# Channel attention and two FFNs on one core: three weight units converted in the head, four leftover groups at other places

## The chip, the cores and the metric

One core of a Trainium2 chip. The metric is the device time of one execution in microseconds (us). TensorE (PE) multiplies, VectorE (DVE) and ScalarE (ACT) do the elementwise work, GpSimd (POOL) helps at a few places, and the queue of SyncE (SP) issues every load and store.

## The reference, cut to what matters

```python
qn = q / (np.linalg.norm(q, axis=1, keepdims=True) + 1e-06)   # q, k, v: (1, 6016, 256)
kn = k / (np.linalg.norm(k, axis=1, keepdims=True) + 1e-06)
s = kn.transpose(0, 2, 1) @ qn / tau                          # 256 x 256
a = softmax(s)                                                # exp(s - max) / (sum + 1e-09)
x = v @ a                                                     # 6016 x 256
h = x @ w_in1;  x = (h * np.clip(h + 3.0, 0.0, 6.0) / 6.0) @ w_out1     # 256 -> 2048 -> 256
h = x @ w_in2;  out = np.maximum(h, 0.0) ** 2 @ w_out2
```

## The kernel before

Every product is made of three passes: operands are split into a high part (a cast on ACT) and a rest (a subtraction on DVE), and PE runs high x high, rest x high, high x rest (`passes`, L310 to L312).

The **head** reads q and k in groups of two blocks of 128 tokens (`GROUPS`, tiles `qk`, tags `wo0` to `wo7`, so 8 buffers, each 512 KB). For every one of 47 blocks ACT squares it into PSUM (L296), DVE adds the square to one of two running sums (L297), and PE adds its outer product to the two halves of `s` (`score`, L300). The last ten blocks' second halves are left for later (`late`, `DEFER`).

Then comes the **chain from the norms to M1**: PE sums over partitions (`nrm`, L385), DVE and ACT make reciprocal norms (L391 to L409), PE spreads them (`rq_ps`, L410), ACT copies that (L417), `softmax(0)` and `softmax(1)` scale, take the maximum and exponentiate, PE transposes (`et_ps`, L437), and ACT and DVE split the transposed result. M1 is the softmax times the first 512 columns of `w_in1` (`m1_half`): four half products of three passes each, 12 matmuls, whose casts and rests (`m1_out`, L476, L478) are the weights `wa_0` that the first FFN multiplies x by. `late` scores stand on PE after `nrm` (six of them, `LATE_AT`) and after `rq_ps` (four). `keep_busy` puts matmuls without use into PE's waits.

The weights arrive as 64-bit floats and are **converted in units**: `unit` loads one and returns five steps, on ACT an absolute value, a copy and at the end a cast of the high part, on DVE two TENSOR_SCALAR, a SCALAR_TENSOR_TENSOR, an integer add (L167) and the rest: five DVE instructions. Units are `wi1_0` to `wi1_7` and `wo1_0` to `wo1_7`. In the head only `wi1_0` is converted (`EARLY`, `EARLY_AT`), `wi1_1` and `wo1_0` stand in the chain, and 13 others in the first pair.

The **first pair** (`steps`) is a loop over 32 steps. A step has one product `h` (6 matmuls), ACT's `r` (L628), DVE's `g` (L630), the split into `gs`, and two groups `acc` (6 matmuls) that lag by `LAG` = 2 steps. `issue` is called twice a step and issues the conversion steps that `START` and `DENSE` put at that place. At steps 5, 13 and 21 another M1 part is made. After the last step four groups are left (`pending`); they are put into free slots of the first unit of the next pair, a Strassen unit (`strassen`) of 15 slots. In that unit the bank `y` collects B11, T2, T1 and B22, and ACT copies it out after each of the first three (`sa`, `su`, `se`, L766) before PE may add the next.

Of the kernel before, what the change touches and what calls it, by code (L numbers as in the profile page):

```python
# [8 lines left out]
F32 = mybir.dt.float32  # L9
# [17 lines left out]
NU = KF // 2  # L27
GROUPS = [1] + [2] * 23
DEFER = 10
LATE_AT = 6  # L30
LAG = 2
AHEAD = 3
BUSY = (6, 2, 2, 3)
M1_LEAD = 3
EARLY = 12
TAU_AT = 20
EARLY_AT = {15: (0, 1), 16: (2,), 18: (3, 4)}


START = [-5, -3, 0, 3, 6] + [9 + 4 * k for k in range(9)]  # L40
DENSE = 5
SIGN = -(2 ** 31)
APART = 2.6
APART_FIRST = 3.2
SLOTS = 15

B11, B21, T2, T3, T1, B22, T4 = range(7)
# [8 lines left out]
def attention_then_two_ffns(  # L56
# [230 lines left out]

    s_ps = [ps_acc.tile([P, C], F32, tag="acc", name=f"s{i}") for i in range(KC)]

    sums = [small(2 * C) for _ in range(2)]  # L290
    for x in sums:
        nc.vector.memset(x, 0.0)

    def squares(t, x):
        sq = bank([P, 2 * C], f"sq{t}")
        nc.scalar.activation(sq, x, AF.Square)  # L296
        nc.vector.tensor_tensor(out=sums[t % 2], in0=sq, in1=sums[t % 2], op=ALU.add)  # L297

    def score(t, x, i):
        nc.tensor.matmul(  # L300
# [13 lines left out]
    with tc.manual_schedule():  # L314
# [8 lines left out]
        pre = []  # L323
        t = 0
        for gi, n in enumerate(GROUPS):
            src = wpool.tile([P, 1024], F32, tag=f"wo{gi % NU}", name=f"qk{gi}")[:, :2 * n * C]
            nc.sync.dma_start(
                out=src.rearrange("p (t x c) -> p t x c", t=n, x=2), in_=qk[:, t:t + n, :, :]
            )
            if gi == EARLY:  # L330
                pre.append(unit("wi1", 0, raw1[0]))
            for st in EARLY_AT.get(gi, ()):
                pre[0][st]()
# [17 lines left out]
        et = [hpool.tile([P, KC, C], F32R, tag="o", bufs=4, name=f"et{s}") for s in ("h", "l")]  # L351

        order = [
            ("wo1", 0), ("wi1", 2), ("wo1", 1), ("wi1", 3), ("wo1", 2), ("wi1", 4), ("wo1", 3), ("wi1", 5),
            ("wo1", 4), ("wi1", 6), ("wo1", 5), ("wi1", 7), ("wo1", 6), ("wo1", 7),
        ]
        loaded = []

        def feed():
            k = len(loaded)  # L360
            if k < len(order):
                which, u = order[k]
                loaded.append(unit(which, u, raw1[u] if which == "wi1" and u < len(raw1) else None))
# [4 lines left out]
            for k in range(KC):  # L368
                nc.sync.dma_start(out=raw[k][:, :, :w], in_=(vt[p] if j == 0 else x2_d[p])[:, 2 * k:2 * k + 2, :w])

        pre.append(unit("wi1", 1, raw1[1]))
        raw0 = [gpool.tile([P, 2, WMAX], F32, tag="g", name=f"v0_{k}") for k in range(KC)]
        load_x(0, 0, raw0)
        for _ in range(AHEAD):
            feed()


        for st in range(4):
            pre[1][st]()


        nrm = ps_acc.tile([P, 4], F32, tag="acc", name="nrm")
        for b in range(4):
            for m, x in enumerate(sums):
# [125 lines left out]
        operands = {}  # L510
        raws = {}

        def operand(j, p, r):

            at = j * NP + p
            if r in (B11, B21) and at % 2:
                t = wpool.tile([P, 2, WMAX], F32R, tag=f"b{2 + r}", name=f"x{j}_{p}_{r}")
            elif r == T2 and at % 2:
                t = ops.tile([P, 2, WMAX], F32R, tag="opx", name=f"x{j}_{p}_{r}")
            else:  # L520
                t = ops.tile([P, 2, WMAX], F32R, tag=f"op{r}", name=f"x{j}_{p}_{r}")
            t = t[:, :, :WIDTHS[p]]
            operands[j, p, r] = [t[:, i, :] for i in range(2)]
            return operands[j, p, r]


        x0 = {}

        def split_first(k):
            w = WIDTHS[0]  # L530
            for n in range(2):
                hi, lo = x0[k, n] = operand(0, 0, ((B11, T3), (B21, B22))[k][n])
                split(hi, lo, raw0[k][:, n, :w])
# [440 lines left out]
```

## Time and profile before

| | |
|---|---|
| median of 3 runs | 1046.49 us (1046.17 to 1046.52) |
| profiled execution | 1046.23 us, of which the span of its instructions is 1044.1 us |
| busy share of the span | PE 99%, DVE 83%, ACT 64%, POOL 3% |
| granted TensorE clock | 1.000 in every slice |
| loads of the head | qk 23 x 512 KB and 1 x 256 KB |

The page's busy shares average over very different stages. PE's 99% counts a matmul until its modelled end, so short waits hardly show in it; they are read from the starts of two matmuls in a row.

### The profile page before, as it was taken

Reading aid. Unit: us, or ns where it says so; the run is one execution under the profiler, and the core shown is the slowest. Engines: PE = TensorE matmul, PEld = TensorE weight load, DVE = VectorE, ACT = ScalarE, POOL = GpSimd, SP = SyncE. Lnnn points to the kernel's source line nnn. Section 1 sums busy time; section 2 is a strip of 40 time slices with the busy share of each in tenths; the row PEclk is TensorE's granted clock in tenths of the full one; section 3 lists DMA queues with packets and bytes.
Section 4 is the critical chain, followed back from the end, with each engine's and each line's share of the span. In section 5 each row is a group of like instructions: output and inputs, shape, how many; then the busy total and the mean of one; then the engine's idle time right before and its main releaser. Section 6 shows DMA issues by size and latency. Waiting matters only on the chain.

```text
span 1044.1 us, 12995 instructions
## 1 busy us (share of the span) xinstructions
PE 1033.6 (99%) x4630; PEld 865.3 (83%) x4630; DVE 863.0 (83%) x1461; ACT 665.6 (64%) x1200; POOL 29.9 (3%) x33
## 2 busy tenths in 40 slices
PE   9999999999999999999999999999999999999998
PEld 8867787888888888888998888888888888888997
DVE  7899868889989989988987788778688678778765
ACT  7687777788878778777876455445455455445443
POOL 0012240000000000000000000000000000000000
PEclk9999999999999999999999999999999999999999
DMA  9911204003403402222665002002001100200100
GB/s 371 344 40 41 81 1 142 1 1 116 157 0 116 156 1 111 82 76 92 227 225 187 1 1 80 1 1 69 13 1 40 42 1 1 75 1 1 41 1 36
DMA packets 25936, 77.64 MB, mean 74 GB/s; under 512 B 2832, under 2 KB 4880, under 8 KB 25872
## 3 DMA queue, kind: packets, MB, share of 16 engines
q1 hardware_dynamic: 25872, 76.82, 21.0%
q8 instruction: 36, 0.59, 0.2%
q14 instruction: 28, 0.23, 0.1%
HBM read 52.95 MB, written 23.86 MB: 74 GB/s over the span
## 4 chain that ended last, share of the span: by engine, by line
PE 88%; DVE 7%; ACT 4%; issue 1%; DMA 1%; SPq 0%; ACTq 0%
PE acc L312 15%; PE acc L311 15%; PE acc L310 15%; PE y L310 7%; PE y L311 7%; PE y L312 7%; PE q L311 4%; PE q L310 4%; PE q L312 4%; PE s L300 3%; PE x L312 2%; PE x L310 2%; PE x L311 2%; DVE gs L125 2%; DVE g L630 1%
## 5 line engine op out<-in xcount | busy, mean ns | idle before, releaser
L125 DVE TENSOR_TENSOR gs<-g,gs 128x512 fp32r<-128x512 f32 (+1 forms) x384 | 260.4, 678 | 55.6 <-ACT gs L793 46.1
L312 PE MATMUL acc<-gs,wo 128*128 128x512 f32 (+1 forms) x768 | 296.8, 386 | 0.8 <-DVE gs L125 0.6
L310 PE MATMUL acc<-gs,wo 128*128 128x512 f32 (+1 forms) x768 | 296.2, 386 | 0.9 <-ACT gs L123 0.9
L311 PE MATMUL acc<-gs,wo 128*128 128x512 f32 (+1 forms) x768 | 295.9, 385 | 0.0
L793 ACT CAST gs<-g 128x512 fp32r<-128x512 f32 (+1 forms) x352 | 208.6, 613 | 31.0 <-DVE g L784 22.0
L312 PEld LDWEIGHTS acc<-gs,wo 128*128 128x128 f32 x768 | 144.2, 188 | 30.8 <-DVE gs L125 4.0
L310 PEld LDWEIGHTS acc<-gs,wo 128*128 128x128 f32 x768 | 144.2, 188 | 28.5 <-ACT gs L123 2.0
L311 PEld LDWEIGHTS acc<-gs,wo 128*128 128x128 f32 x768 | 144.2, 188 | 26.6
L766 ACT COPY se<-y 128x512 f32<-128x512 f32 (+1 forms) x88 | 50.7, 576 | 121.3 <-PE y L312 121.2
L770 DVE TENSOR_TENSOR h<-q,se 128x512 f32<-128x512 f32 (+1 forms) x88 | 59.5, 676 | 63.1 <-ACT se L766 62.6
L766 ACT COPY su<-y 128x512 f32<-128x512 f32 (+1 forms) x88 | 50.7, 576 | 87.1 <-PE y L312 76.4
L789 DVE SCALAR_TENSOR_TENSOR g<-h 128x512 f32<-128x512 f32 (+1 forms) x144 | 97.0, 673 | 0.0
L776 ACT ACTIVATE r<-h,three 128x512 f32<-128x512 f32 (+1 forms) x120 | 85.5, 713 | 8.6 <-DVE h L770 8.2
L784 DVE SCALAR_TENSOR_TENSOR g<-r,h 128x512 f32<-128x512 f32 (+1 forms) x120 | 80.6, 672 | 3.8 <-ACT r L776 3.8
L778 ACT ACTIVATE r<-y 128x512 f32<-128x512 f32 (+1 forms) x48 | 28.3, 590 | 62.7 <-PE y L312 62.7
L770 DVE TENSOR_TENSOR h<-q,su 128x512 f32<-128x512 f32 (+1 forms) x88 | 59.4, 675 | 1.4
L770 DVE TENSOR_TENSOR h<-x,sa 128x512 f32<-128x512 f32 (+1 forms) x88 | 59.1, 672 | 0.0
L766 ACT COPY sa<-y 128x512 f32<-128x512 f32 (+1 forms) x88 | 50.7, 576 | 6.8 <-PE y L312 0.7
L789 DVE SCALAR_TENSOR_TENSOR g<-y,r 128x512 f32<-128x512 f32 (+1 forms) x48 | 32.7, 681 | 23.7 <-ACT r L778 23.1
L300 PE MATMUL s<-qk 128*128 128x256 f32 x188 | 41.7, 381 | 0.8 <-DMA qk<-in_qk 0.8
L300 PEld LDWEIGHTS s<-qk 128*128 128x128 f32 x188 | 35.5, 191 | 6.1 <-DMA qk<-in_qk 1.5
L310 PE MATMUL y<-x,wa_0h 128*128 128x512 f32 (+1 forms) x88 | 34.0, 386 | 0.7 <-ACT se L766 0.7
(241 smaller groups left out, 1761.6 us busy)
## 6 DMA issues: line engine op xcount, KB each, us to landing
qk<-in_qk SPq DMA_DIRECT2D x23, 512.0 KB, 7.0
wo<-in_w_out SPq DMA_DIRECT2D x16, 512.0 KB, 5.2
wi<-in_w_in SPq DMA_DIRECT2D x10, 512.0 KB, 4.6
x2d<-o SPq DMA_DIRECT2D x20, 256.0 KB, 2.4
raw<-x2d SPq DMA_DIRECT2D x10, 512.0 KB, 5.6
out<-o SPq DMA_DIRECT2D x20, 256.0 KB, 2.2
raw<-in_vt SPq DMA_DIRECT2D x8, 512.0 KB, 5.9
wo2d<-wo2s SPq DMA_DIRECT2D x8, 512.0 KB, 2.9
```

Source lines behind the costliest of these rows:

```text
L125: eng.tensor_tensor(out=lo, in0=x, in1=f32(hi), op=ALU.subtract)
L300: nc.tensor.matmul(s_ps[i], lhsT=x[:, C + i * P:C + (i + 1) * P], rhs=x[:, :C], start=(t == 0), stop=(t == NT - 1))
L310: nc.tensor.matmul(ps, lhsT=ah, rhs=bh, start=first, stop=False, skip_group_check=more)
L311: nc.tensor.matmul(ps, lhsT=al, rhs=bh, start=False, stop=False, skip_group_check=more)
L312: nc.tensor.matmul(ps, lhsT=ah, rhs=bl, start=False, stop=last, skip_group_check=more)
L766: nc.scalar.copy(s[tag], s["y"])
L770: nc.vector.tensor_tensor(out=s[which], in0=s[ps], in1=s[tag], op=ALU.add)
L776: nc.scalar.activation(s["r" + which], h, AF.Relu, bias=three)
L778: nc.scalar.activation(s["r" + which], h, AF.Relu)
L784: nc.vector.scalar_tensor_tensor(out=g, in0=s["r" + which], scalar=6.0, in1=h, op0=ALU.min, op1=ALU.mult)
L789: nc.vector.scalar_tensor_tensor(out=g, in0=h, scalar=0.0, in1=r, op0=ALU.max, op1=ALU.mult)
L793: nc.scalar.copy(gs[which][0], s["g" + which])
```

## The change

`wi1_0`, `wi1_1` and `wo1_0` are all converted in the head, and loaded between the qk groups 6 and 7, 9 and 10, 12 and 13. The qk tiles keep off tag `wo0` (it now holds `wo1_0`), so they have 7 buffers. The squares of 13 blocks go to SBUF and are added by POOL to a third sum, which DVE adds to the first one at block 41. The table load for Exp stands right behind the square root. Two of the four splits of the first x stand before the norms, one after `rest(0)`, one after M1. Both transposes stand before M1 on PE. The third `keep_busy` goes, and `late` is divided five and five. In the first pair 13 units are issued as before, in another order and at other places, and the four leftover groups stand at slots 1, 8, 11, 12 instead of 3, 4, 6, 8.

```diff
-LATE_AT = 6
+LATE_AT = 5
-BUSY = (6, 2, 2, 3)
+BUSY = (6, 2, 2)
-EARLY = 12
+EARLY = ((6, "wi1", 0), (9, "wi1", 1), (12, "wo1", 0))
+EARLY_AT = (3, 3, 4, 5, 6)
-EARLY_AT = {15: (0, 1), 16: (2,), 18: (3, 4)}
+POOL_UNTIL = 39
+JOIN = 41
-START = [-5, -3, 0, 3, 6] + [9 + 4 * k for k in range(9)]
-DENSE = 5
+START = [-1, 2, 5, 8, 11, 14, 17, 22, 26, 30, 34, 39, 45]
+DENSE = 3
+LEFT_AT = (1, 8, 11, 12)
...
     def squares(t, x):
+        if t % 3 == 1 and t < POOL_UNTIL:
+            sq = hpool.tile([P, 2 * C], F32, tag="r", name=f"sq{t}")
+            nc.scalar.activation(sq, x, AF.Square)
+            nc.gpsimd.tensor_tensor(out=sums[2], in0=sq, in1=sums[2], op=ALU.add)
+        else:
...
+        if t == JOIN:
+            nc.vector.tensor_tensor(out=sums[0], in0=sums[2], in1=sums[0], op=ALU.add)
...
-            src = wpool.tile([P, 1024], F32, tag=f"wo{gi % NU}", name=f"qk{gi}")[:, :2 * n * C]
+            src = wpool.tile([P, 1024], F32, tag=f"wo{1 + gi % (NU - 1)}", name=f"qk{gi}")[:, :2 * n * C]
...
         order = [
-            ("wo1", 0), ("wi1", 2), ("wo1", 1), ("wi1", 3), ("wo1", 2), ("wi1", 4), ("wo1", 3), ("wi1", 5),
-            ("wo1", 4), ("wi1", 6), ("wo1", 5), ("wi1", 7), ("wo1", 6), ("wo1", 7),
+            ("wi1", 2), ("wi1", 3), ("wo1", 1), ("wo1", 2), ("wi1", 4), ("wi1", 5), ("wo1", 3), ("wo1", 4),
+            ("wi1", 6), ("wo1", 5), ("wi1", 7), ("wo1", 6), ("wo1", 7),
         ]
...
-        pre.append(unit("wi1", 1, raw1[1]))
...
-        for st in range(4):
-            pre[1][st]()
+        split_first(0)
...
         nc.scalar.activation(root, x2n, AF.Sqrt, scale=2.0 ** -10)
-        pre[1][4](0)
+        nc.scalar.activation(warm, ones[:, 0:1], AF.Exp)
+        loaded[0][0]()
...
         e0 = softmax(0)
         keep_busy(BUSY[1], "busy1")
-        loaded[0][2]()
         transposed(0, *e0)
         e1 = softmax(1)
-        loaded[0][3]()
-        loaded[0][4](0)
+        row_sums(0, *e0)
         rest(0, *e0)
-        loaded[0][4](1)
-        feed()
-        row_sums(0, *e0)
+        split_first(1, 0)
         keep_busy(BUSY[2], "busy2")
-        m1_half(0, 0, 0)
         transposed(1, *e1)
         rest(1, *e1)
         row_sums(1, *e1)
+        m1_half(0, 0, 0)
         m1_half(0, 0, 1)
-        for k in range(KC):
-            split_first(k)
-        loaded[1][0]()
+        split_first(1, 1)
         m1_out(0, 0)
...
-        free = sorted(set(range(SLOTS)) - {x % SLOTS for x in PLACE})
-        for x, go in zip(free, [(n, f, d, gs) for n, f, gs in pending for d in range(KC)]):
+        for x, go in zip(LEFT_AT, [(n, f, d, gs) for n, f, gs in pending for d in range(KC)], strict=True):
```

How the instructions stand, at three places. ACT from the square root to the first cast of the transposed softmax, before (`tbwo`, `tywo`, `wi1h` are steps of units, `rq_ps` the spread norms, `eth` the cast):

```order
L393 ACTIVATE scratch_110<-scratch_110 128x4
L123 CAST wi1h_356<-tawi_1_435 128x512
L154 ACTIVATE tbwo_0_469<-wo_0_430 128x512
L157 ACTIVATE tywo_0_470<-wo_0_430 128x512
L415 ACT_TABLE_LOAD
L415 ACTIVATE scratch_110<-both 128x1
L417 COPY scratch_110<-rq_ps 128x256
L431 ACTIVATE scratch_111,scratch_110<-scratch_110 128x256
L438 CAST eth<-et_ps_489 128x256
```

And the same stretch after the change, from the first two casts of x on:

```order
L129 CAST x_0_0_461<-v_0_453 128x512
L129 CAST x_0_3_464<-v_0_453 128x512
L431 ACTIVATE scratch_110<-scratch_110 128x4
L432 ACT_TABLE_LOAD
L432 ACTIVATE scratch_110<-both 128x1
L160 ACTIVATE tbwi_2_485<-raw12h 128x512
L452 COPY scratch_111<-rq_ps 128x256
L466 ACTIVATE scratch_111,scratch_110<-scratch_111,scratch_110 128x256
L473 CAST eth<-et_ps_507 128x256
```

Three unit steps of 512 columns between the square root and the copy became one, and the table load moved ahead of it. DVE from the first `g` of the first pair to the second, before:

```order
L630 SCALAR_TENSOR_TENSOR g_0_0_592<-r_0_0_590,h_0_0_576 128x512
L167 ISA tawi_2_539<-tawi_2_539,tywi_2_541 128x1024
L125 TENSOR_TENSOR gs_0_0_599<-g_0_0_592,gs_0_0_599 128x512
L125 TENSOR_TENSOR wi1l_603<-tawi_2_539,wi1h_602 128x512
L158 TENSOR_SCALAR tawo_1_595<-wo_1_433 128x512
L159 TENSOR_SCALAR tbwo_1_596<-tbwo_1_596 128x512
L630 SCALAR_TENSOR_TENSOR g_0_1_613<-r_0_1_611,h_0_1_580 128x512
```

And after:

```order
L630 SCALAR_TENSOR_TENSOR g_0_0_586<-r_0_0_584,h_0_0_570 128x512
L164 TENSOR_SCALAR tawi_2_484<-raw12h 128x512
L165 TENSOR_SCALAR tbwi_2_485<-tbwi_2_485 128x512
L131 TENSOR_TENSOR gs_0_0_591<-g_0_0_586,gs_0_0_591 128x512
L168 SCALAR_TENSOR_TENSOR tawi_2_484<-tbwi_2_485,tawi_2_484 128x512
L630 SCALAR_TENSOR_TENSOR g_0_1_597<-r_0_1_595,h_0_1_574 128x512
```

One full-width unit instruction fewer stands between the two. PE in the first Strassen unit, from T3 (bank `q`) to B22 (the last `y` product), before; `acc_0` are the leftover groups:

```order
L310 MATMUL q_1_0_1533<-x_1_3_1497,wa_0h 128x512
L311 MATMUL q_1_0_1533<-x_1_3_1497,wa_0l 128x512
L312 MATMUL q_1_0_1533<-x_1_3_1497,wa_0h 128x512
L310 MATMUL acc_0_1_1_712<-gs_1_15_1486,wo_7_1324 128x512
L311 MATMUL acc_0_1_1_712<-gs_1_15_1486,wo_7_1324 128x512
L312 MATMUL acc_0_1_1_712<-gs_1_15_1486,wo_7_1324 128x512
L310 MATMUL y_1_0_1493<-x_1_4_1436,wa_0h 128x512
L311 MATMUL y_1_0_1493<-x_1_4_1436,wa_0l 128x512
L312 MATMUL y_1_0_1493<-x_1_4_1436,wa_0h 128x512
L310 MATMUL y_1_0_1493<-x_1_5_1516,wa_0h 128x512
```

And after, from T1 to B22:

```order
L325 MATMUL y_1_0_1491<-x_1_4_1434,wa_0h 128x512
L323 MATMUL acc_0_1_0_697<-gs_1_15_1484,wo_7_1366 128x512
L324 MATMUL acc_0_1_0_697<-gs_1_15_1484,wo_7_1366 128x512
L325 MATMUL acc_0_1_0_697<-gs_1_15_1484,wo_7_1366 128x512
L323 MATMUL acc_0_1_1_701<-gs_1_15_1484,wo_7_1366 128x512
L324 MATMUL acc_0_1_1_701<-gs_1_15_1484,wo_7_1366 128x512
L325 MATMUL acc_0_1_1_701<-gs_1_15_1484,wo_7_1366 128x512
L323 MATMUL y_1_0_1491<-x_1_5_1514,wa_0h 128x512
```

Two leftover groups, six matmuls, now stand between T1 and B22, where none stood.

## Rows read from the trace of the kernel before

**Rows 1.** Chain that ended last, in the head: start us, us, what.

```profile
7.68 33.94 PE s L300 x156
```

**Rows 2.** Timeline 41 to 59: start, us, engine, line, operation, count [idle before <-releaser].

```profile
41.46 1.84 PE L385 MATMUL nrm<-both,scratch 128*128 128x1 f32 x16
43.16 2.84 PE L300 MATMUL s<-qk 128*128 128x256 f32 x12
44.87 0.48 DVE L409 TENSOR_SCALAR scratch<-both,scratch 128x128 f32<-128x128 f32 x2
45.41 1.28 ACT L415 ACT_TABLE_LOAD   x1
45.84 0.61 PE L410 MATMUL rq_ps<-scratch,both 128*128 128x128 f32 x4
46.81 0.36 ACT L417 COPY scratch<-rq_ps 128x256 f32<-128x256 f32 x1
48.18 0.51 ACT L431 ACTIVATE scratch<-scratch 128x256 f32<-128x256 f32 x1 [1.01 <-DVE scratch L428]
48.88 0.41 PE L437 MATMUL et_ps<-both,scratch 128*128 128x128 f32 x2 [0.26 <-issue]
51.84 2.18 ACT L123 CAST x<-v 128x512 fp32r<-128x512 f32 x4
54.50 0.47 ACT L476 ACTIVATE wa_0h<-mp,rs 128x256 fp32r<-128x256 f32 x1
55.02 0.50 PE L310 MATMUL h<-x,wa_0h 128*128 128x512 f32 x1 [0.47 <-ACT wa_0h L476]
57.17 0.39 PE L310 MATMUL h<-x,wa_0h 128*128 128x512 f32 x1
58.31 0.39 PE L312 MATMUL h<-x,wa_0h 128*128 128x512 f32 x1
```

**Rows 3.** Timelines of DVE, ACT and SP in the head.

```profile
4.18 0.69 DVE L297 TENSOR_TENSOR scratch<-sq,scratch 128x512 f32<-128x512 f32 x1 [2.24 <-ACT sq L296]
...
35.72 4.86 DVE L297 TENSOR_TENSOR scratch<-sq,scratch 128x512 f32<-128x512 f32 x8
35.72 3.18 ACT L296 ACTIVATE sq<-qk 128x512 f32<-128x512 f32 x6
28.74 3.78 SPq L327 DMA_DIRECT2D qk<-in_qk  x3
33.05 0.90 SPq L369 DMA_DIRECT2D v<-in_vt  x2
```

**Rows 4.** Stretch 8 to 24: us, busy by engine, clock, DMA share, GB/s; then tile v.

```profile
8.00:24.00 16.00, 16.00 (x76) 14.08 (x75) 14.46 (x24) 13.16 (x24) 0.00 (x0) 1.00 1.02 415
DMA to landing us min/median/max: 7.5/7.9/8.3
```

**Rows 5.** Timeline of DVE: first and last of four steps of one unit.

```profile
40.50 0.41 DVE L158 TENSOR_SCALAR tawi<-raw11l 128x512 int32<-128x512 int32 x1
42.11 0.69 DVE L167 CUSTOM_DVE_ANT_0 tawi<-tawi,tywi 128x1024 uint16<-128x1024 uint16 x1
```

**Rows 6.** Timelines of POOL and DVE where both work.

```profile
113.57 2.58 POOL L125 TENSOR_TENSOR wa_1l<-m,wa_1h 128x512 fp32r<-128x512 f32 x2 [17.68 <-ACT wa_1h L123]
114.63 0.69 DVE L630 SCALAR_TENSOR_TENSOR g<-r,h 128x512 f32<-128x512 f32 x1 [0.90 <-ACT r L628]
60.22 1.21 DVE L125 TENSOR_TENSOR gs<-g,gs 128x512 fp32r<-128x512 f32 x1
```

**Rows 7.** Stretch of the first pair: us, PE busy (matmuls), clock, DMA share, GB/s.

```profile
55.00:160.30 105.30, 102.66 (x434) 1.00 0.14 46
```

**Rows 8.** Waits 55 to 160: engine, line, waited for: us in total, times, longest.

```profile
PEld acc L312 <- DVE gs L125: 2.7, 5, 0.8
PEld acc L310 <- ACT gs L123: 2.0, 3, 0.9
```

**Rows 9.** Timeline of PE where the first Strassen unit changes to B22.

```profile
160.31 0.39 PE L312 MATMUL y<-x,wa_0h 128*128 128x512 f32 x1
161.38 0.50 PE L310 MATMUL y<-x,wa_0h 128*128 128x512 f32 x1 [0.68 <-ACT se L766]
```

More of the change, by code (lines that the diff above doesn't have):

```diff
@@ L288, in attention_then_two_ffns @@
     s_ps = [ps_acc.tile([P, C], F32, tag="acc", name=f"s{i}") for i in range(KC)]
-    sums = [small(2 * C) for _ in range(2)]
+    sums = [small(2 * C) for _ in range(3)]
     for x in sums:
@@ L294, in squares @@
     def squares(t, x):
-        sq = bank([P, 2 * C], f"sq{t}")
-        nc.scalar.activation(sq, x, AF.Square)
-        nc.vector.tensor_tensor(out=sums[t % 2], in0=sq, in1=sums[t % 2], op=ALU.add)
+        if t % 3 == 1 and t < POOL_UNTIL:
[3 more added lines that the diff above has]
+        else:
+            sq = bank([P, 2 * C], f"sq{t}")
+            nc.scalar.activation(sq, x, AF.Square)
+            nc.vector.tensor_tensor(out=sums[t % 2], in0=sq, in1=sums[t % 2], op=ALU.add)
+        if t == JOIN:
+            nc.vector.tensor_tensor(out=sums[0], in0=sums[2], in1=sums[0], op=ALU.add)
     def score(t, x, i):
@@ L329, in attention_then_two_ffns @@
             )
[L330 to L333, printed above, removed]
+            for i, (x, which, u) in enumerate(EARLY):
+                if gi == x:
+                    pre.append(unit(which, u, raw1[u] if which == "wi1" else None))
+                for st, after in enumerate(EARLY_AT):
+                    if gi == x + after:
+                        pre[i][st]()
             if gi == TAU_AT:
@@ L375, in attention_then_two_ffns, with operand, split_first @@
             feed()
-        for st in range(4):
-            pre[1][st]()
+        operands = {}
+        raws = {}
+        def operand(j, p, r):
+            at = j * NP + p
+            if r in (B11, B21) and at % 2:
+                t = wpool.tile([P, 2, WMAX], F32R, tag=f"b{2 + r}", name=f"x{j}_{p}_{r}")
+            elif r == T2 and at % 2:
+                t = ops.tile([P, 2, WMAX], F32R, tag="opx", name=f"x{j}_{p}_{r}")
+            else:
+                t = ops.tile([P, 2, WMAX], F32R, tag=f"op{r}", name=f"x{j}_{p}_{r}")
+            t = t[:, :, :WIDTHS[p]]
+            operands[j, p, r] = [t[:, i, :] for i in range(2)]
+            return operands[j, p, r]
+        x0 = {}
+        def split_first(k, *halves):
+            w = WIDTHS[0]
+            for n in halves or range(2):
+                hi, lo = x0[k, n] = operand(0, 0, ((B11, T3), (B21, B22))[k][n])
+                split(hi, lo, raw0[k][:, n, :w])
+        split_first(0)
         nrm = ps_acc.tile([P, 4], F32, tag="acc", name="nrm")
         for b in range(4):
-            for m, x in enumerate(sums):
+            for m, x in enumerate(sums[:2]):
                 nc.tensor.matmul(
@@ L405, in attention_then_two_ffns @@
         rq_ps = ps_acc.tile([P, C], F32, tag="acc", name="rq_ps")
-        loaded[0][0]()
         for i in range(KC):
@@ L412, in attention_then_two_ffns @@
             score(*a)
-        pre[1][4](1)
-        loaded[0][1]()
-        nc.scalar.activation(warm, ones[:, 0:1], AF.Exp)
         rq = small(C)
@@ L507, in m1_sums_split @@
             split(hi, lo, m1_st[c4][:, u, :, :], part, idle_first(c4 < 2))
[L510 to L533, printed above, removed]
         e0 = softmax(0)
         keep_busy(BUSY[1], "busy1")
-        loaded[0][2]()
         transposed(0, *e0)
         e1 = softmax(1)
-        loaded[0][3]()
-        loaded[0][4](0)
+        row_sums(0, *e0)
         rest(0, *e0)
-        loaded[0][4](1)
-        feed()
-        row_sums(0, *e0)
+        split_first(1, 0)
         keep_busy(BUSY[2], "busy2")
-        m1_half(0, 0, 0)
         transposed(1, *e1)
@@ L559, in attention_then_two_ffns @@
         m1_keep(0)
-        loaded[1][1]()
-        loaded[1][2]()
-        keep_busy(BUSY[3], "busy3")
         x2_d = [dram.tile([P, 4, WMAX], F32, name=f"x2d{p}") for p in range(NP)]
```

## The prediction

> **What bounds the kernel now.** The page says little, since PE counts as busy almost everywhere. So I read first the chain that ended last: in the head it is PE's scores alone, 156 passes without a gap from 7.68 us [rows 1], so loads, squares and sums hide behind PE there. From 41.46 on the timeline shows another picture: PE waits for a chain of small instructions, and the first product `h` starts at 55.02 [rows 2]. Of these 13.6 us useful work is little: 16 passes `nrm` (1.7 by the start of the next row), 20 late scores at (45.84 - 43.16) / 12 = 0.22, that is 4.4, `rq_ps` and the transposes about 0.45 each, and M1's 12 matmuls. A matmul of 512 columns takes (58.31 - 57.17) / 5 = 0.228 when nothing waits [rows 2], so M1 is 2.7. That makes 9.7; some 3.9 us are waits or fillers.
>
> The third look is at the first pair, by stretch: 434 matmuls from 55 to 160.3 [rows 7], at 0.228 make 99.0 of 105.3 us, so PE stands about 6.3 us there, 0.7 of it in the first `h` products (12 matmuls from 55.02 that end at 58.31 + 0.23 = 58.54 instead of 57.76). The waits name DVE and ACT, the split of `g` above all [rows 8]. Where the first Strassen unit goes from T1 to B22, PE's starts are 1.07 apart: 0.84 lost to the copy `se` [rows 9].
>
> **The change part by part.**
>
> *Loads.* Two more units, 1.05 MB, now come ahead of the last qk group. Before, SP issued the last three groups in steps of about 1.72, the last near 32.2 [rows 3]; that is PE's pace for a group (8 passes at 0.2155), since an issue waits for PE to release a buffer. With 7 buffers instead of 8 it waits for one group more: the last issue moves by 1.72. ACT ended the squares at 38.90 before, DVE the adds at 40.58 [rows 3], DVE being the later one with eight adds in a row at 0.61. After, the last square ends at 38.90 + 1.72 = 40.6 at the latest by this step, and one add behind it is done at 41.25. PE starts `nrm` at 41.46 anyway [rows 2]. So I take 0.0, between nothing and 0.6. The x loads are issued right behind the last group, now without `wi1_1` between, which gave back one load's time; they landed 7.5 and 8.3 after issues at 33.05 and 33.51 [rows 3, 4], at 40.6 and 41.8, and I expect the first by 41.0 to 42.3. Its two casts (0.55 each, of the four in 2.18 [rows 2]) and the rest behind them then end between 42.7 and 44.0; DVE is wanted for the norms at 43.2, when `nrm` is through, so at the late end 0.8 would be lost. I take nothing.
>
> The Trainium skill, page "SBUF — State Buffer", section "Summary: rules for kernel authors", says to plan with about 358 GB/s between HBM and SBUF. The 13.9 MB up to the last group would by it take an estimated 38.8 us, and land near 41 with the first bytes' delay, so that the norms would start about 1.2 later. The trace does not agree: the same queue moved 415 GB/s from 8 to 24 us [rows 4].
>
> *Sums.* 13 of 47 adds go to POOL. POOL takes 1.29 for a 128 x 512 add [rows 6]; one is due every three blocks, 2.6 us, so it has half its time free. DVE loses 13 x 0.61 = 7.9 and gets one add (0.6) and two units. A unit is four instructions in 2.3 (40.50 to 42.80 [rows 5]) and a rest of 0.6 to 0.7, so 5.9 for two. DVE has 1.4 less to do in the head: nothing by itself, since PE is the bound.
>
> *Norms to the Exp.* Before, ACT's copy of `rq_ps` started at 46.81, behind the table load that ends at 46.69, though `rq_ps` was made from 45.84 on [rows 2]. After, the load stands behind the square root and runs while DVE works. With five late scores PE is free at 43.16 + 10 x 0.2155 = 45.3, just when DVE ends the diagonals (44.87 + 0.48). So the copy can start near 46.1, 0.7 earlier, and the Exp that ended at 48.69 ends at 48.0. PE takes part of that back: the other five late scores run from 45.85 to 48.0, two fillers (0.45) behind them, so the transposes start at 48.45 instead of 48.88 [rows 2]: 0.4 gained.
>
> *Transposes to the products.* Before, from 48.88 to 55.02 are 6.1 us. In them M1 stands between the two transposes, ACT makes four casts of x from 51.84, and an absolute value, and so comes to M1's own cast only at 54.50 [rows 2]. After: transposes at 48.45, cast, second Exp to 49.8, second transposes 50.0 to 50.4, then M1's 12 matmuls in one run to 53.15. Of the x casts one stands before the second `eth` and one after it, so ACT is free at 51.4 and casts `wa_0` as soon as the first six matmuls are through, at 52.0 to 52.75; DVE's rests follow to 53.5. `h` starts at 53.15. The second half's cast (to 54.0) and rest (to 54.7) come as its products are reached, so the four products end at 53.15 + 12 x 0.228 = 55.9, against 58.54. **Gain 2.6**, between 1.5 (sums or x 0.6 late, and half a microsecond lost between cast and rest) and 3.2.
>
> *First pair.* The 13 units left there are as many DVE instructions as before. Between the first and the second `g`, DVE has one full-width instruction less, and it comes to the first `g` without the rests of x (four, 0.6 each) just behind it. The second `g` should so come about 1.2 earlier still, and the waits for `gs` of the first steps shrink. The rows have 4.7 us of load waits for `gs` in all [rows 8]; a few of the early ones, 1.1, should go (between 0.2 and 1.7). Later units stand further apart from place 17 on, for which I take 0.2.
>
> *Leftover groups.* Two groups, 1.37 us, now stand between T1 and B22 and cover the copy that cost 0.84 [rows 9]. T2 has T3 and a group behind it, and B11 a group and B21, also 1.37 each, over a copy of 0.6 with its latencies. I take 0.75 (0.4 to 0.84).
>
> **Sum:** 2.6 + 1.1 + 0.2 + 0.75 = 4.65. From the profiled execution's 1046.23 that gives 1041.6; the median of the runs is 0.26 above it, so I predict 1041.8.
>
> **The rivals.** A difference of 0.2%, 2.1 us, is about what a measurement of this kernel can tell from no change.
>
> *The last loads come late.* If an issue in a full queue takes 7.5 us as the x loads did [rows 4], the last group (issued at 33.9) lands at 41.4, is squared by 42.6 and added by 43.2: `nrm` starts 1.7 later, and the result is 1043.5. Against it: the queue is PE's pace at the end, not full. The figure of the Trainium skill's page above would do the same here.
>
> *DVE stays the bound of the first pair.* Per step it has two instructions of 0.61 for `g` and `gs`; a unit every three places, that is 1.5 steps, adds 3.0 / 1.5 = 2.0, so 3.2 against PE's 12 x 0.228 = 2.7. This density now lasts to place 17, before it thinned out from 9. Then PE gets to the products earlier and waits for `gs` all the more: the 1.3 of the pair are not gained, perhaps 0.7 more is lost, and it ends at 1043.1 to 1043.8. For it: the waits in rows 8. Against it: the M1 parts give DVE 2.7 us of PE time for few instructions.
>
> *The chain does not shorten.* If what ends last between the norms and `h` is something left as it was (the late scores on PE, the row from Exp to Exp), only half of the 2.6 comes and some of the pair's, near 1044.6: no change that can be measured.
>
> *POOL blocks DVE: slower.* A rest with both inputs in SBUF took 1.21 instead of 0.69 while POOL worked; a `g`, with one input in PSUM, kept 0.69 beside a POOL add [rows 6]. The sums' adds read the square from PSUM, like `g`, so they should be free. If they were blocked for all of POOL's time, 13 x 1.29 = 16.8 us, DVE would have about 34 x 0.61 + 0.6 + 3 x 3.0 + 16.8 = 47.1 us of work from 4.2 on [rows 3], and end at 51.3 instead of 41.3. That costs 10 and gives 4.65: 1051.8. The point from which it decides: DVE has 6.8 us to spare (37.1 - 30.3), so blocked time beyond 11.4 us makes the kernel slower.
>
> **How the numbers follow.** My forecast has 0.56, late loads 0.12, DVE in the pair 0.16, the chain 0.09, POOL 0.04, and 0.03 for something else slower. Forecast and late loads, and most of DVE in the pair, lie below 1044.4, the bound for faster: 0.81. No change: 0.12. Slower: 0.07. The forecast's own range goes from the sum with the upper gains (3.2 + 1.7 + 0.4 + 0.84 = 6.1: 1040.4) to that with a head of 1.5 and little from the pair (1043.5). The range for 8 in 10 goes a little below, 1039.8, since PE stands 6.3 us in the pair and more of that may go than I took, and up to 1044.4, which takes in late loads and DVE in the pair.
>
> **What would show it.** In the changed profile: `nrm` at 41.4 to 41.7; the sums' adds still at 0.61 to 0.69 with POOL's beside them; the table load ending before 45.3; the transposes at 48.4 to 48.6; M1's 12 matmuls in one run; `h` from about 53.2, its four products done by 56; fewer and shorter waits of `acc` for `gs` before 75; no gap above 0.3 before B22. Wrong it would be by `nrm` after 42.2, by adds of 1.2 on DVE, or by a product `h` that starts on time while the first Strassen unit does not come 4 us earlier.

## The result and the profile after

The change made the kernel slower: 1053.76 us as the median of 5 runs (1051.41 to 1057.58), against 1046.49 of before in the same session; the ratio is 1.0075, 95% interval 1.0064 to 1.0086. The prediction, 1041.8 and "faster", was wrong in its sign. The profiled execution took 1053.53 us, its span is 1051.7 at a mean granted clock of 0.997.

First some marks, PE's starts in us by the timelines of PE in both profiles (of before, `nrm` and `h` stand in [rows 2], B22 in [rows 9]):

| | before | after | difference so far |
|---|---|---|---|
| `nrm` | 41.46 | 44.79 | +3.33 |
| first `h` | 55.02 | 59.64 | +4.62 |
| first four products done | 58.54 | 62.62 | +4.08 |
| second M1 part begins | 70.96 | 74.32 | +3.36 |
| third M1 part begins | 96.64 | 104.37 | +7.73 |
| fourth M1 part begins | 123.96 | 131.85 | +7.89 |
| first Strassen unit | 154.42 | 162.99 | +8.57 |
| B22 | 161.38 | 169.11 | +7.73 |

So there are two large losses: one before `nrm` and just behind it, and one of 4.37 in a single stretch of the pair. Between them the difference shrinks three times (0.54, 0.72 and, at B22, 0.84), where the prediction had gains. PE's timeline of the changed kernel from the last scores of the head to the first `h` (start, us, engine, line, what, count, and in brackets the idle time before it and who ended it):

```profile
40.55 1.13 PE L313 MATMUL s<-qk 128*128 128x256 f32 x4
44.79 2.91 PE L423 MATMUL nrm<-both,scratch 128*128 128x1 f32 x16 [3.12 <-DVE scratch L308]
47.56 4.61 PE L313 MATMUL s<-qk 128*128 128x256 f32 x10
51.97 0.81 PE L448 MATMUL rq_ps<-scratch,both 128*128 128x128 f32 x4
52.62 2.32 PE L313 MATMUL s<-qk 128*128 128x256 f32 x10
59.64 0.39 PE L323 MATMUL h<-x,wa_0h 128*128 128x512 f32 x1
```

PE stands for 3.12 us and waits for DVE's last sum (L308). Then ten late scores take (51.97 - 47.56) / 10 = 0.44 each, twice the 33.94 / 156 = 0.218 of the head [rows 1]; the ten behind `rq_ps` are at 0.22 again. Stretches of the same profile (us, then busy us and instructions of PE, PEld, DVE, ACT, POOL, the granted clock, DMA share, GB/s):

```profile
4.00:17.30 13.30, 12.83 (x59) 10.93 (x58) 7.15 (x11) 8.95 (x17) 6.35 (x5) 1.00 1.00 388
17.30:44.80 27.50, 24.37 (x113) 20.80 (x111) 26.86 (x41) 22.43 (x42) 12.02 (x10) 1.00 1.00 392
44.70:52.00 7.30, 7.21 (x27) 6.31 (x28) 2.74 (x11) 2.24 (x4) 0.00 (x0) 0.56 0.68 280
```

And of before:

```profile
4.00:17.30 13.30, 12.53 (x58) 10.44 (x57) 10.91 (x18) 9.92 (x19) 0.00 (x0) 1.00 1.02 400
17.30:40.60 23.30, 23.30 (x110) 20.51 (x109) 20.87 (x36) 18.25 (x34) 0.70 (x1) 1.00 0.99 363
```

Up to 17.3 DVE now has almost half its time free; behind it, from the first unit's steps on, it is busy for 26.86 of 27.50 us, and PE pays. From 44.7 to 52.0 PE's granted clock is 0.56, almost all of it the lower of its two levels, 1.2 instead of 2.4 GHz. DVE's timeline in the head shows what fills it:

```profile
17.99 1.33 DVE L165 TENSOR_SCALAR tbwi<-tbwi 128x512 f32<-128x512 f32 x1
...
31.04 1.29 DVE L308 TENSOR_TENSOR scratch<-sq,scratch 128x512 f32<-128x512 f32 x2
32.25 1.80 DVE L168 SCALAR_TENSOR_TENSOR tawo<-tbwo,tawo 128x512 int32<-128x512 int32 x1
33.98 0.68 DVE L308 TENSOR_TENSOR scratch<-sq,scratch 128x512 f32<-128x512 f32 x1
34.58 1.15 DVE L173 CUSTOM_DVE_ANT_0 tawo<-tawo,tywo 128x1024 uint16<-128x1024 uint16 x1
38.47 2.48 DVE L308 TENSOR_TENSOR scratch<-sq,scratch 128x512 f32<-128x512 f32 x4 [0.17 <-ACT sq L307]
41.66 3.08 DVE L308 TENSOR_TENSOR scratch<-sq,scratch 128x512 f32<-128x512 f32 x5
```

The same two kinds of unit step before:

```profile
26.50 0.42 DVE L159 TENSOR_SCALAR tbwi<-tbwi 128x512 f32<-128x512 f32 x1
28.35 0.68 DVE L162 SCALAR_TENSOR_TENSOR tawi<-tbwi,tawi 128x512 int32<-128x512 int32 x1
```

The adds keep their 0.6 to 0.7, but the units' steps, 0.42 to 0.69 before, take up to 1.80 beside POOL:

```profile
32.23 1.28 POOL L304 TENSOR_TENSOR scratch<-sq,scratch 128x512 f32<-128x512 f32 x1 [2.37 <-ACT sq L303]
33.79 1.39 POOL L304 TENSOR_TENSOR scratch<-sq,scratch 128x512 f32<-128x512 f32 x1 [0.28 <-ACT sq L303]
```

ACT stands behind that step too: its cast of the unit waits 2.12 us, and the squares, next in its program, come behind the cast.

```profile
35.76 0.62 ACT L129 CAST wo<-tawo 128x512 fp32r<-128x512 f32 x1 [2.12 <-DVE tawo L173]
36.29 1.11 ACT L307 ACTIVATE sq<-qk 128x512 f32<-128x512 f32 x2
```

In the pair, the stretch that lost most is around 100. PE waits twice for `gs`, which by its starts costs 3.3 of the 4.37; the rest is in short waits at 83 to 85 and 95 to 96:

```profile
99.39 0.50 PE L323 MATMUL acc<-gs,wo 128*128 128x512 f32 x1 [0.87 <-ACT gs L129]
101.97 0.50 PE L325 MATMUL acc<-gs,wo 128*128 128x512 f32 x1 [1.84 <-DVE gs L131]
```

On DVE a stretched unit step stands ahead of `g`, and three more between it (97.54) and its `gs` (101.24):

```profile
95.82 1.79 DVE L173 CUSTOM_DVE_ANT_0 tawi<-tawi,tywi 128x1024 uint16<-128x1024 uint16 x1
97.54 0.67 DVE L630 SCALAR_TENSOR_TENSOR g<-r,h 128x512 f32<-128x512 f32 x1
98.31 1.26 DVE L131 TENSOR_TENSOR wi1l<-tawi,wi1h 128x512 fp32r<-128x512 f32 x1
99.49 0.96 DVE L164 TENSOR_SCALAR tawo<-wo 128x512 int32<-128x512 int32 x1
100.38 0.94 DVE L165 TENSOR_SCALAR tbwo<-tbwo 128x512 f32<-128x512 f32 x1
101.24 0.68 DVE L131 TENSOR_TENSOR gs<-g,gs 128x512 fp32r<-128x512 f32 x1
```

POOL forms M1's sums (L222) beside them:

```profile
97.02 1.20 POOL L222 TENSOR_TENSOR m<-m 128x256 f32<-128x256 f32 x1
98.30 0.73 POOL L222 TENSOR_TENSOR m<-m,m 128x256 f32<-128x256 f32 x1
```

### The profile page after: what moved, and what is told of

Read it like the earlier page. It is cut to its first block, busy times and chain, and to the rows that moved or that the text cites. A ratio compares the mean times of both kernels' runs of the same rounds, so it can differ in the third digit from the quotient of the medians.

```text
span 1051.7 us, 12972 instructions
## 1 busy us (share of the span) xinstructions
PE 1036.1 (99%) x4624; PEld 867.1 (82%) x4624; DVE 862.4 (82%) x1450; ACT 665.4 (63%) x1200; POOL 46.5 (4%) x46
## 4 chain that ended last, share of the span: by engine, by line
PE 87%; DVE 7%; ACT 3%; issue 1%; DMA 1%; SPq 0%; ACTq 0%; DVEq 0%
PE acc L325 15%; PE acc L323 15%; PE acc L324 15%; PE y L323 7%; PE y L324 7%; PE y L325 7%; PE q L323 4%; PE q L325 4%; PE q L324 4%; PE x L325 2%; PE x L323 2%; PE x L324 2%; DVE gs L131 2%; DMA qk<-in_qk 1%; PE s L313 1%
## 5 line engine op out<-in xcount | busy, mean ns | idle before, releaser
L131 DVE TENSOR_TENSOR gs<-g,gs 128x512 fp32r<-128x512 f32 (+1 forms) x384 | 261.0, 680 | 56.1 <-ACT gs L793 46.0
L313 PE MATMUL s<-qk 128*128 128x256 f32 x188 | 44.3, 397 | 0.5 <-DMA qk<-in_qk 0.5
L776 ACT ACTIVATE r<-y,three 128x512 f32<-128x512 f32 (+1 forms) x40 | 26.9, 673 | 11.8 <-PE y L325 11.0
```

The source lines that it names most:

```text
L313: nc.tensor.matmul(s_ps[i], lhsT=x[:, C + i * P:C + (i + 1) * P], rhs=x[:, :C], start=(t == 0), stop=(t == NT - 1))
L776: nc.scalar.activation(s["r" + which], h, AF.Relu, bias=three)
```

## The experiments

My first theory: the loss is DVE's, behind 17.3 us; late sums make PE stand, its clock falls, and both are paid. Rivals: POOL's share is what costs; the new order of the chain costs; the pair costs by its density. Each kernel ran 5 to 11 times. The profile of each is of one execution, and its time need not be the median.

**1. PE kept busy before `nrm`.** Sixteen matmuls without use.

```diff
-        nrm = ps_acc.tile([P, 4], F32, tag="acc", name="nrm")
+        nrm = ps_acc.tile([P, P], F32, tag="acc", name="nrm")
+        for _ in range(16):
+            nc.tensor.matmul(nrm, lhsT=ones, rhs=ones, start=True, stop=True)
...
-        nc.vector.tensor_scalar_max(x2n, nrm, 1e-30)
+        nc.vector.tensor_scalar_max(x2n, nrm[:, :4], 1e-30)
```

> The changed kernel, with 16 matmuls without use ahead of nrm (3.5 us of PE, written into the tile that nrm overwrites), which fill PE's wait for the last sum. Theory 'idle PE, then a lower clock': in the changed profile PE stood still from 41.5 to 44.8 and the granted clock was 0.56 from 44.7 to 52; with the wait filled, nrm still starts near 44.8, but the clock stays at 1.00, nrm and the late scores take 1.8 and 2.2 instead of 2.9 and 4.4, h starts 3 to 3.5 us earlier (about 56.3) and the time falls by about 3, to 1050.5, with a smaller spread between runs. Rival 'the lower clock comes from the stretch as a whole, or from elsewhere': the clock stays near 0.56 there and the time stays within 1 us of the changed kernel's.

Measured: 1051.83, ratio to before 1.0050 (1.0037 to 1.0062). The sums end no earlier (44.94), but the late scores run at full pace:

```profile
45.02 1.92 PE L425 MATMUL nrm<-both,scratch 128*128 128x1 f32 x16
46.80 2.40 PE L313 MATMUL s<-qk 128*128 128x256 f32 x10
49.04 0.61 PE L450 MATMUL rq_ps<-scratch,both 128*128 128x128 f32 x4
56.51 0.39 PE L323 MATMUL h<-x,wa_0h 128*128 128x512 f32 x1
```

`h` starts 3.1 earlier than after the change and the profiled execution is 3.06 shorter; the median is only 1.9 lower, and the changed kernel's runs spread over 6. So the fallen clock is a term of its own. It also lets the chain be read at full clock: `nrm` to `h` is 11.5 us.

**2. POOL's share of the sums undone** in the changed kernel.

```diff
-POOL_UNTIL = 39
-JOIN = 41
+POOL_UNTIL = 0
+JOIN = -1
```

> The changed kernel with all 47 squares added on DVE again; the three units stay in the head. Theory 'port': POOL's adds stretched DVE's two-source unit steps (up to 1.80 instead of 0.68), ACT waited behind them in order, and so the last sum came 3.3 us late; without POOL's adds these steps are back at 0.68 to 0.69, the sums end by 43.0, nrm starts by 43.1, and the time falls by 1.5 to 5. Rival 'load': three units and 47 adds are 38 us of DVE's work and more than it has, so the sums end at 45 or later and the time is the same or 1 to 3 us longer. Rival 'late loads': the last qk group lands at 40.5 as before, and nrm can't start before 42.4 in either case.

Measured: 1052.5 (1.0065, 1.0052 to 1.0078). `nrm` is at 44.08, the second to third M1 part takes 30.10. With 12 adds more on DVE the head is 0.7 shorter, not longer. The units' steps are back at 0.42 to 0.68, and the sums are late all the same: POOL's share is not the cause of the loss, but neither does it relieve anything. DVE alone is full:

```profile
17.30:30.00 12.70, 12.70 (x60) 11.19 (x59) 12.48 (x23) 10.66 (x20) 0.00 (x0) 1.00 1.02 416
30.00:44.00 14.00, 11.62 (x54) 9.80 (x52) 14.00 (x26) 12.12 (x23) 0.53 (x1) 1.00 0.94 357
```

**3. The leftover groups alone**, in the kernel before.

```diff
-        for x, go in zip(free, [(n, f, d, gs) for n, f, gs in pending for d in range(KC)]):
+        for x, go in zip((1, 8, 11, 12), [(n, f, d, gs) for n, f, gs in pending for d in range(KC)]):
```

> The kernel before with nothing changed but the four leftover groups at slots 1, 8, 11, 12. From the term of the prediction: 0.4 to 0.84 us faster, 1045.7, and the gap of 1.07 between T1 and B22 is gone. Rival 'given back': the groups leave other waits of the unit open and the time is the same within 0.2.

Measured: 1045.4 against 1046.34 (0.9991, 0.9982 to 1.0000). The groups run between T1 and B22, and the gap of [rows 9] is gone:

```profile
158.81 0.39 PE L312 MATMUL y<-x,wa_0h 128*128 128x512 f32 x1
159.03 0.39 PE L310 MATMUL acc<-gs,wo 128*128 128x512 f32 x1
...
160.17 0.39 PE L312 MATMUL acc<-gs,wo 128*128 128x512 f32 x1
160.39 0.39 PE L310 MATMUL y<-x,wa_0h 128*128 128x512 f32 x1
```

B22 comes 0.99 earlier than before, of which 0.15 stood already at the first Strassen unit (154.27 against 154.42): the switch gains 0.84. By the median the kernel is 0.94 faster, with the interval's edge at no change.

**4. A thinner pair.** The same list, units four places apart from place 12 on.

```diff
-START = [-1, 2, 5, 8, 11, 14, 17, 22, 26, 30, 34, 39, 45]
+START = [-1, 2, 5, 8] + [12 + 4 * k for k in range(9)]
```

> The changed kernel, with the units from the fourth on at places 4 apart (12, 16, ... 44) instead of 11, 14, 17, 22, ... Theory 'density': between the first two M1 parts the changed kernel lost 4.4 us, 3 of them in two waits near 98 and 100 where POOL and crowded unit steps meet on DVE; with units 4 apart the stretch from the first to the second M1 part shrinks by 2 to 4 us, and the time by as much. Rival 'collision': the wait depends on where POOL's sums happen to meet DVE, not on the density, so it moves or stays and the stretch changes by less than 1 us.

Measured: 1054.09 (1.0080, 1.0066 to 1.0094). The lost stretch is back to 25.90, where before had 25.68; but a unit is now too late for the last M1 part, and PE waits for it:

```profile
131.83 0.50 PE L323 MATMUL mp<-wi1h,eth 128*128 128x512 f32 x1 [3.24 <-ACT wi1h L129]
```

That the places of the units' steps cause the stretch's loss is shown by this; the time is not better, and the new wait is as long as most of what the stretch gained.

**5. The pair in the order of before** (`wi1` and `wo1` in turn), with nearly its distances.

```diff
-START = [-1, 2, 5, 8, 11, 14, 17, 22, 26, 30, 34, 39, 45]
-DENSE = 3
+START = [-1, 1, 4, 7, 10, 13, 17, 21, 25, 29, 33, 37, 41]
+DENSE = 4
...
-            ("wi1", 2), ("wi1", 3), ("wo1", 1), ("wo1", 2), ("wi1", 4), ("wi1", 5), ("wo1", 3), ("wo1", 4),
+            ("wi1", 2), ("wo1", 1), ("wi1", 3), ("wo1", 2), ("wi1", 4), ("wo1", 3), ("wi1", 5), ("wo1", 4),
```

> The changed kernel, with the 13 units of the first pair in the order of the kernel before (wi1 and wo1 in turn) and from the fifth on 3 or 4 places apart, none of wi1 later than there. Theory 'density': between the first and the second M1 part the changed kernel needs 30.1 us, the kernel before 25.7; here it is 25.5 to 27, from the second to the third about 27.3 (before 27.3), and the time falls by 3 to 5 from 1053.8, to about 1049.5. Rival 'start late': the pair loses because its DVE work begins 4 us later against PE, not by the places; the stretches stay at 29 or more and the time stays within 1 us.

Measured: 1051.5 (1.0051, 1.0039 to 1.0064), 2.3 below the changed kernel; the first Strassen unit starts at 160.33 instead of 162.99, the lost stretch takes 28.17. Both are less than I expected (3 to 5, and 25.5 to 27).

**6. Two units in the head instead of three**; `wo1_0` opens the pair's list, which so has 14 units and other places (the lines of its new order are not shown).

```diff
-EARLY = ((6, "wi1", 0), (9, "wi1", 1), (12, "wo1", 0))
+EARLY = ((6, "wi1", 0), (9, "wi1", 1))
...
-START = [-1, 2, 5, 8, 11, 14, 17, 22, 26, 30, 34, 39, 45]
-DENSE = 3
+START = [-1, 2, 5, 8, 11, 14, 18, 21, 25, 28, 32, 35, 39, 44]
+DENSE = 4
...
```

> The changed kernel with two units converted in the head instead of three (wo1_0 goes first in the pair, 14 units there). Theory 'DVE's work after the loads': from group 9's landing at 17.3 the changed kernel has 26.9 us of DVE work before the norms, and DVE is busy 26.86 of the 27.5 us to 44.8; POOL's adds before 17.3 helped nothing. A unit less is 3 us of DVE work and its waits for POOL less, so the last sum ends at 41.5 to 42.5, nrm starts by 42.6, PE's wait is about 1 us, and the granted clock up to h stays at 0.97 or more; h starts by 54.5. Rival 'port or loads': taking a unit out moves the last sum by less than 1 us, nrm starts at 43.5 or later.

Measured: 1049.3 (1.0029, 1.0018 to 1.0041). The sums end at 42.75 instead of 44.74, `nrm` starts at 42.81: one unit is 2.0 of the 3.33. What ends the sums is no longer DVE's work. The last qk group, issued at 34.08, lands 6.67 later, and ACT stands for it:

```profile
40.83 1.12 ACT L307 ACTIVATE sq<-qk 128x512 f32<-128x512 f32 x2 [1.92 <-DMA qk<-in_qk]
```

So behind DVE's work the late loads wait as a second bound; by themselves they put `nrm` 1.35 later than before. The clock fell here too, which I had not expected, behind a wait of 0.89 for DVE (`nrm` to `rq_ps` 5.72, before 4.38 [rows 2]). A wait of 2.98 for `wo1_0` at 64.86 is this kernel's own, and hides what else it would gain.

**7. POOL's adds later**, every second block from 17 to 43.

```diff
-POOL_UNTIL = 39
-JOIN = 41
+POOL_UNTIL = 44
+JOIN = 45
...
-        if t % 3 == 1 and t < POOL_UNTIL:
+        if t % 2 == 1 and 16 < t < POOL_UNTIL:
```

> The changed kernel with POOL's adds moved: instead of every third block up to 37, every second one from 17 to 43 (14 instead of 13), so that POOL helps only after the units' steps begin; blocks before 17 are DVE's. Theory 'DVE's work after the loads': DVE then has 16 adds, three units and the join after 17.3, 19.4 us and some 3 to 5 of waits for POOL: the last sum ends at 41.5 to 42.8 and nrm starts by 42.9 instead of 44.8. Rival 'port': twice as many POOL adds beside the units' two-source steps stretch them more, and the sums end at 44.5 or later.

Measured: 1053.77 (1.0069, 1.0057 to 1.0082), `nrm` at 45.42. My theory had 42.9 at the latest, so its forecast failed, and the rival's number came. As a test of DVE's load it is inconclusive: ACT waited for the two buffers that POOL reads (0.52 before the square at 41.17), and DVE, which waited for squares between its last adds (0.35 to 0.95 at a time), for POOL ahead of the joining add (0.26 at 43.88). The kernel's own waits cover the question.

**8. Experiments 1 and 5 together.**

> Both repairs that were tried apart: the 16 matmuls without use ahead of nrm, and the pair's units in the order and about at the places of the kernel before. If the causes add up: head to h 3.1 to 3.3 and pair 3 to 5 less than the changed kernel's 1053.8, so 1045.5 to 1047.5, within 1 us of the kernel before. Rival 'one cause': the two share their gain (a pair that starts earlier collides as before), and the time is 1048.5 or more.

Measured: 1049.18 (1.0026, 1.0016 to 1.0036), in two groups: four runs of 1047.37 to 1048.09 at a granted clock of 1.000, five of 1049.18 to 1050.9 at 0.998 or 0.999. I had expected 1045.5 to 1047.5. In the profiled one, of the second group, the sums ended at 46.03, the filler was too short, and PE waited 0.86; the ten late scores then took 0.32 each, the clock falling among them. The first group suggests that the gains add where the filler reaches; no profile of that group was taken, so this is not shown.

**9. Two units, and the gaps of the chain used as before.** The qk tiles get their eighth buffer back, the pair its order of before (the lines of both are not shown), and `wo1_0` is converted between the norms and M1.

```diff
-EARLY = ((6, "wi1", 0), (9, "wi1", 1), (12, "wo1", 0))
+EARLY = ((6, "wi1", 0), (9, "wi1", 1))
...
-START = [-1, 2, 5, 8, 11, 14, 17, 22, 26, 30, 34, 39, 45]
-DENSE = 3
+START = [-5, -1, 1, 3, 6] + [9 + 4 * k for k in range(9)]
+DENSE = 5
...
         nc.scalar.copy(rq, rq_ps)
+        loaded[0][1]()
...
         e0 = softmax(0)
+        loaded[1][0]()
...
         e1 = softmax(1)
+        loaded[0][2]()
...
         rest(0, *e0)
+        loaded[0][3]()
...
+        loaded[0][4](0)
+        loaded[0][4](1)
+        feed()
         m1_out(0, 1)
```

> Two units in the head instead of three, qk back to 8 buffers, and the steps of wo1_0 in gaps of the chain as before the change; the pair has the list of units of before at nearly its places. Kept: POOL's share of the sums, the new order from the norms to M1, the leftover groups at their new places. If the loss is DVE's work behind 17.3 us and what follows from it (late sums, PE idle, clock), then nrm comes at 41.5 to 42.2, PE's clock stays at 1.00 from 41 to 52, h starts at 53 to 54, the pair runs at the pace of before and the switch to Strassen gains 0.8: 1043 to 1044, faster than both kernels. If instead the new order of the chain or POOL's share of the sums costs by itself, nrm is at 42.5 or later or h not before 55, and the time is 1047 or more.

Measured: 1046.58 against 1046.48 (1.0000, 0.9991 to 1.0009). My 1043 to 1044 was wrong: DVE still ends the sums at 42.34, PE waits 1.04 and the scores go at half pace.

```profile
42.40 2.53 PE L423 MATMUL nrm<-both,scratch 128*128 128x1 f32 x16 [1.04 <-DVE scratch L308]
44.79 4.61 PE L313 MATMUL s<-qk 128*128 128x256 f32 x10
49.19 1.06 PE L448 MATMUL rq_ps<-scratch,both 128*128 128x128 f32 x4
```

The stretch from 44 to 52, granted clock 0.60:

```profile
44.00:52.00 8.00, 8.00 (x28) 6.86 (x28) 3.17 (x12) 3.54 (x7) 0.00 (x0) 0.60 0.30 123
```

The eleven runs fall in two groups by the clock of the whole execution: three at 1.000 took 1044.62 to 1045.51, eight at 0.997 or 0.998 took 1046.51 to 1048.05. The profiled one is of the second group.

**10. The same without POOL's share of the sums** (experiment 2's edit on 9).

> The kernel before this one, with all 47 sums on DVE. If POOL's share relieves DVE, DVE has 12 adds of 0.61 more, 6 of them behind 17.3 us, the last sum ends near 42 to 43, nrm moves by 0.5 to 2 and the time by as much or, with the clock falling after it, by up to 4. If POOL's work in the head only stretches DVE's steps by as much as it takes over, the two are equal within 0.5.

Measured: 1044.69 (1043.31 to 1045.49), ratio 0.9981, 0.9973 to 0.9990: the only version here whose whole interval is on the faster side, by 1.8 us. Neither of my readings had that sign. DVE ends the sums at 42.15, hardly earlier than in 9, though it adds 12 squares more; PE goes into `nrm` without a wait, and its clock stays at 1.00 (0.999 or 1.000 for the whole execution in all eleven runs, which are as fast as the three of experiment 9 that kept theirs):

```profile
39.70 2.54 PE L313 MATMUL s<-qk 128*128 128x256 f32 x11
42.20 1.95 PE L423 MATMUL nrm<-both,scratch 128*128 128x1 f32 x16
44.01 2.40 PE L313 MATMUL s<-qk 128*128 128x256 f32 x10
46.25 0.61 PE L448 MATMUL rq_ps<-scratch,both 128*128 128x128 f32 x4
54.11 0.40 PE L323 MATMUL h<-x,wa_0h 128*128 128x512 f32 x1
```

The stretch from 41.9 to 52:

```profile
41.90:52.00 10.10, 9.44 (x57) 8.10 (x56) 7.49 (x23) 6.64 (x15) 0.00 (x0) 1.00 0.83 314
```

That `nrm` is at 42.20 and not at 41.46 is here PE's doing, not DVE's: its scores end only then, and 0.6 of the 0.74 is the third qk group, which landed at 8.26 instead of 7.64. So in this profile a late start of PE helped to hide the end of the sums, 42.15. That all eleven runs kept the clock speaks against mere luck, but why no wait arises here, where eight of the eleven runs of experiment 9 lost some of their clock, is not shown.

**11. POOL's share alone**, in the kernel before (13 adds and the joining one).

> The kernel before the change with POOL's 13 adds and the joining add alone. In that kernel PE is the bound until 41.4, and DVE has time to spare with one unit, so by the theory of DVE's load nothing happens: nrm within 0.3 of 41.46, time within 1 of before. If POOL beside DVE is itself what makes the change slow, the sums end later than 40.6, nrm comes at 42 or later, and the time is 2 or more above before.

Measured: 1046.9 against 1046.48 (1.0001, 0.9992 to 1.0010), `nrm` at 41.31. With one unit DVE has idle time that hides the two steps that POOL stretched:

```profile
25.91 1.38 DVE L161 TENSOR_SCALAR tbwi<-tbwi 128x512 f32<-128x512 f32 x1
28.41 1.56 DVE L164 SCALAR_TENSOR_TENSOR tawi<-tbwi,tawi 128x512 int32<-128x512 int32 x1
```

## Why the prediction was wrong, step by step

**The step that failed first** is in *Sums*: "DVE has 1.4 less to do in the head: nothing by itself, since PE is the bound", and with it the 6.8 us "to spare". Both were counted over the whole head. But squares can't be added before they land, and the units' steps begin only behind 17.3: of the idle time of before, 13.30 - 10.91 = 2.4 us lay ahead of that and 23.30 - 20.87 = 2.4 behind it. POOL, with one block in three from the start on, took five of its 13 adds in the early part, where they saved idle time. Behind 17.3 the sum is: two units more, 5.9; eight adds fewer and one joining add, 8 x 0.61 - 0.6 = 4.3 saved; the time by which POOL stretched steps between 17.5 and 35.7, which by the timeline is 0.91 (L165), 0.36, 0.48 and 0.47 (L173), twice 0.32 (L131) and 1.12 (L168), 4.0. That is 5.6 more; by the stretches DVE is busy 26.86 - 20.87 = 6.0 longer. It still idles for 0.6 of the 2.4, and so the last sum ends 4.16 later, at 44.74 instead of 40.58; before, the sums were 0.83 ahead of `nrm`, and 3.33 is left. Experiments 6 (a unit less: 2.0) and 2 (no POOL, no stretched step, and DVE full) bear it out. The stretched steps are a reading of the timelines, which experiment 11 repeats with one unit. The sign that I gave for being wrong, `nrm` after 42.2, came. The second step that failed is in *First pair*, below: a gain of 0.2 where 4.37 was lost.

**POOL and DVE.** I looked at the port only for the sums' adds, which read PSUM, and those stayed at 0.68 as I said. What I put at nothing is the units' own steps beside POOL. The rows in [rows 6] had the warning: a rest with two SBUF inputs took 1.21 there. That the rival on POOL gave 1051.8, near the measured time, is luck: it had the adds blocked, for 10 us, where the adds were not blocked and the other steps lost 4.0. The Trainium skill, page "SBUF — State Buffer", section "SBUF: two separate sides", says that a DVE operation with two SBUF inputs (where the GpSimd operation reads SBUF), or in a mode that uses both ports, and a GpSimd operation exclude each other for a whole instruction. The trace agrees for two inputs: 0.68 became 1.80 beside a POOL add of 1.28. TENSOR_SCALAR with one input went from 0.42 to 1.33; that it runs in such a mode no run here shows.

**Loads.** Expected 0.0 to 0.6 late. The last qk group was issued at 33.69 (I had 33.9) and landed at 40.50, against 37.70 before, near the 41.4 of the rival. SP did issue the last three groups at PE's pace, as before, but that the queue is "not full" was wrong: it moved 392 GB/s from 17.3 to 44.8 (363 before, to 40.6). The last issue moved by 1.5, near the 1.72 that I had, but I moved the squares by no more than that, and the group also took 6.8 instead of 5.5 to land. Experiment 6 shows what this is worth when DVE is not the bound: `nrm` 1.35 late, near the rival's 1.7. In the changed kernel the group landed 0.25 earlier than there, so by an estimate about 1.1 of the 3.33 would be left if only DVE's work went; DVE's work and the late loads overlap, and the two shares do not add.

**The clock** was no step at all. I had `nrm` late at no more than its own price; a PE that stands before it pays again. After the change the ten scores lost 4.41 - 10 x 0.218 = 2.2 and `nrm` 2.77 - 1.70 = 1.1, together 3.3; in experiment 1 `h` comes 3.1 earlier.

**Norms to the products, gain 2.6: right.** In experiment 1, at full clock, the four products end 14.5 behind `nrm` (59.49 - 45.02), before 17.08: 2.6. After the change they end 17.83 behind it, 3.3 of which is the clock.

**First pair, gain 1.1 early and 0.2 later: half right, then wrong in sign.** From the products' end to the second M1 part it took 11.70 instead of 12.42, a gain of 0.72. Then 30.05 instead of 25.68. The sentence on later units that "stand further apart" looked at the end of the table; up to place 17 they stand closer and in another order. The rival on DVE in the pair had the mechanism (waits for `gs`), and a price of 0.7, a sixth of what came. Experiment 4 shows that the places decide, and experiment 2, with the same 30.10, that POOL's adds in the head have no part in it; which part is density and which is that POOL's sums for M1 meet two-source steps there stays open.

**Leftover groups, 0.75: right**: from the first Strassen unit to B22 it took 6.12 instead of 6.96, 0.84 less, after the change and in experiment 3 alone.

The terms together: 3.3 late sums + 3.3 clock - 2.6 chain - 0.7 early pair + 4.4 + 0.2 + 0.7 in the pair's later parts - 0.8 switch = 7.8, against 7.73 at B22 and 7.3 in the profiled time.

## What to carry to other kernels

Count an engine's spare time by the stretch in which the added work can run, not over a stage: DVE's 4.8 us of idle time in the head were worth at most 2.4, because the other half lay ahead of the data. Moving adds to POOL was no relief here, since DVE's other steps took longer beside POOL: look at each form that runs beside it, not only at the one that moves. When the first bound is taken away, look for the one behind it: here it was the last load. And where TensorE waits just before a serial chain, price the wait twice, since the matmuls behind it may run at the lower clock, as they did here; a filler for exactly that wait got most of it back.

## What the hardware showed that was not expected

- A wait of PE of 0.86 to 3.12 us ahead of `nrm`'s sixteen one-column passes was followed by scores at 0.32 to 0.44 instead of 0.22 (after, and experiments 6, 8, 9: granted clock 0.56 and 0.60 in the stretches after and of 9, mostly the 1.2 GHz level). Without a wait (before, experiments 1 and 10) the same passes were followed by scores at full pace. Not every such wait has this effect: behind the two in the pair, 0.87 and 1.84, the clock stayed at 1.00 after the change, and behind the same two, 0.86 and 1.83, it fell in experiment 1 (0.72 from 98.0 to 102.4). What decides is open.
- Loads issued alike land apart: the third qk group, issued at 1.64 or 1.65 in every profile, landed between 6.95 and 8.26, and where PE waits for it the scores behind it start that much later (7.68 before, 8.30 in experiment 10). The last group took 4.3 to 6.8 us from issue to landing; why is open.
